# Row maxima of attention scores from a difference and a relu, and exponentials in 32 and 16 bits by key tile

## The chip, the core and the metric

The kernel runs on one core of a Trainium2 chip. The metric is the device time of one execution in microseconds (us); lower is better. The engines are named as the profile names them: PE is TensorE (PEld its weight loads), DVE is VectorE, ACT is ScalarE, POOL is GpSimd, SP is SyncE, which only issues DMAs here. Each engine works through its own queue in program order and waits for others by semaphores.

## The reference

Three layers follow each other. First comes attention inside clusters, then a layer that takes the largest of three products, then a layer of eight experts. The change lies in attention, and touches one buffer of the second layer.

```
q, k, v: (2 batches, 8 heads, 768, 64); centroids: (8 heads, 16, 64)
q_assign = argmax(normalized q @ normalized centroids);  k_assign likewise
scores = where(q_assign == k_assign, q @ k.T / 8, -1e9)
attn = exp(scores - max(scores, -1));  attn /= sum(attn) + 1e-9
x = attn @ v                                  # as (1536, 512)
h = max(x @ w1, x @ w2, x @ w3);  x = h @ w_out        # w: 512 x 768
... experts on x (1536 tokens, 8 experts, 512 -> 1024 -> 512)
```

## The kernel before

**Steps.** Attention is written as 96 steps: 16 heads (batch 0 first, `hp` counts pairs of heads, `j` is 0 or 1 in the pair) times 6 key tiles `kt` of 128 keys. `attention` calls for each step: `tick` (what was put off until now: the maxima of the step before, then small jobs by due time), `scores`, `values` of the step two earlier (`LAG`), the events of that step, and `spare`. What stands first in this program order stands first in each engine's queue.

**Row maxima.** Each step also takes the row maxima of one query tile, 11 steps ahead (`LEAD`): `row_max` has PE multiply one tile of 128 queries with all 768 keys, as two products of 384 into two PSUM banks (line 440), and DVE reduces each bank to one column (L447). The products carry the cluster mask as additional rows of the operands `A` (`Aq`, `Ak`), so a masked key is far below the others. After the sixth tile `shift` (L459 and on) joins the two columns, POOL turns the maxima into 16-bit rows `mq`, and those are turned (by PE or by a DMA) into rows of `Aq`, so that the next product with `Aq` has the maximum already subtracted.

**Scores and values.** `scores` forms the transposed scores of a key tile in two halves of 384 queries, each by two products (L497: the high parts `A`, then the cross terms `C`), and ACT takes the exponential into `p` (L500). For `j = 0` the values are multiplied in 32 bits: `values` issues six products of `p` with 65 columns of `v` (each shows as two rows of the trace). For `j = 1` ACT makes a 16-bit copy `ph` (L510), DVE the remainder `pl` (L511, issued in the next step), and `values` issues 18 16-bit products. All collect in the bank `acc`; `norm` divides (L557 to L560).

**Preparation of a pair.** `prep` returns named jobs: `qk` loads, `Hk`, `Hq`, `Lk`, `Lq` split q and k in 16-bit halves, `ck` and `cq` score the clusters, `f1`, `f2`, `f3` pick the first best cluster (`f1` and `f3` on POOL, L347 and L356 to L359), `mk` and `mq` bring the mask rows into `Ak` and `Aq`, `lv` loads v, `vh` halves it, `pv` has PE sum v over all keys (`totals`, six 32-bit products, L408). The table `CF['T']` gives the step of each job, relative to the pair's first step; `CF['E']` gives other steps for the first two pairs.

**What lies between.** During batch 1's steps one unit of the second layer is issued per step (`UP`; a unit is 12 products of 384 columns, L810, then DVE's maximum L818), and its weights are unpacked from 64-bit words, by three of their pieces per step (`QN`): DVE L718 to L742, ACT L720 and L738, POOL L722 and L737. The rest of the second layer and the experts follow when attention has ended.

**PSUM.** Eight banks: row maxima use three in turn in batch 0 and two from step 53 on, scores two.

Of the kernel before, what the change touches and what calls it, by code (L numbers as in the profile page):

```python
# [22 lines left out]
       'Lk': -26,  # L23
       'Lq': -25,
       'ck': -24,
       'cq': -23,
       'ha': -20,
       'mk': -16,
       'mq': -18,
       'lv': -8,  # L30
       'vh': -3,
       'pv': 5,
       'f1': -19,
       'f2': -19,
       'f3': -19},
 'E': [{'Hk': -29,
# [22 lines left out]
        'mq': -7}],  # L59
# [23 lines left out]
 'LAG': 2}  # L83
# [10 lines left out]
C_SGN = 128  # L94
# [13 lines left out]
def constants():  # L108
# [22 lines left out]
class Kernel:  # L131
# [145 lines left out]
    def prep(self, st):  # L277
# [68 lines left out]
        def first1():  # L346
            nc.gpsimd.tensor_tensor(c["eq"], c["eq"], rk, op=ALU.mult)  # L347
# [5 lines left out]
        def first3():  # L353

            eq = c["eq"]
            nc.gpsimd.tensor_tensor(eq, b16(c["mr"]), rk, op=ALU.subtract)  # L356
            nc.gpsimd.tensor_scalar(eq[:, :2 * NT], eq[:, :2 * NT], 0.0, -1.0, op0=ALU.is_equal, op1=ALU.add)
            for i, dst in enumerate((self.AK, self.AQ)):
# [3 lines left out]
                    (61440.0, 0.0)[i], (0.0, 61440.0)[i], op0=(ALU.mult, ALU.is_equal)[i], op1=(ALU.add, ALU.mult)[i])  # L362
# [22 lines left out]

        def load_v():

            st["v"] = v = self.pl.tile([128, NT, 129], F32, tag="v", name=f"v{nm}")
            nc.gpsimd.memset(v[:, :, 64:65], 2.0 ** -10)
            src = I["vP"][b, hp].rearrange("p (t j d) -> p t j d", t=NT, j=2)  # L390
            for j in range(2):
                nc.sync.dma_start(out=v[:, :, 65 * j:65 * j + 64], in_=src[:, :, j, :])


        def v_halves():
            v = st["v"][:, :, 65:129]
# [13 lines left out]

        def split(pv):
            vsh = self.sm.tile([128, 129], F16, tag="vsh", name=f"vsh{nm}", bufs=1)
# [41 lines left out]
    def shift(self, st, j, m2):  # L454
# [3 lines left out]
        mx = self.sm.tile([128, NT], F32, tag="mx", name=f"mx{nm}", bufs=1)  # L458
        nc.vector.tensor_tensor(mx, m2[:, :, 0], m2[:, :, 1], op=ALU.max)  # L459
# [8 lines left out]
            mq[:, :, j, 40:42], mx.unsqueeze(2).to_broadcast([128, NT, 2]), -(2.0 ** 32), (1.0, 1024.0)[j],  # L468
# [19 lines left out]
    def scores(self, st, j, kt, between):  # L488
# [35 lines left out]
    def values(self, st, j, kt, p, plo):  # L524
# [3 lines left out]
        A = st["A"]  # L528
# [944 lines left out]
```

## Time and profile before

| | us |
|---|---|
| median of 3 runs | 552.56 (548.95 to 554.25) |
| the profiled execution | 551.87 |
| its span, first to last instruction | 550.0 |
| PE busy | 475.8 (87%) |
| DVE busy | 424.2 (77%) |
| ACT busy | 289.0 (53%) |
| POOL busy | 140.2 (25%) |

Busy time is the union of an engine's instructions. A product of PE appears with its whole length, from its first column in to its last result out, so products overlap in the trace and a busy PE isn't a PE at its peak; what a step takes from PE is read from start to start. "Idle before" is the time that an engine stood before instructions of a group, and the releaser is what ended it. The mean granted clock of TensorE was 0.974.

### The profile page before, as it was taken

Reading aid. Unit: us, or ns where it says so; the run is one execution under the profiler, and the core shown is the slowest. Engines: PE = TensorE matmul, PEld = TensorE weight load, DVE = VectorE, ACT = ScalarE, POOL = GpSimd, SP = SyncE. Lnnn points to the kernel's source line nnn. Section 1 sums busy time; section 2 is a strip of 40 time slices with the busy share of each in tenths; the row PEclk is TensorE's granted clock in tenths of the full one; section 3 lists DMA queues with packets and bytes.
Section 4 is the critical chain, followed back from the end, with each engine's and each line's share of the span. In section 5 each row is a group of like instructions: output and inputs, shape, how many; then the busy total and the mean of one; then the engine's idle time right before and its main releaser. Section 6 shows DMA issues by size and latency. Waiting matters only on the chain.

```text
span 550.0 us, 11644 instructions
## 1 busy us (share of the span) xinstructions
PE 475.8 (87%) x4518; PEld 326.4 (59%) x4518; DVE 424.2 (77%) x834; ACT 289.0 (53%) x491; POOL 140.2 (25%) x191
## 2 busy tenths in 40 slices
PE   2589898979879879997998899899999999797392
PEld 1258585858657557755775576555666654465271
DVE  5576979797999998999979943462788775989471
ACT  5255757484944744464456444311666632667460
POOL 3513140323145334724433410000000001412122
PEclk9989999999999999999999999899999999989796
DMA  8637494866859334742532133317488843699810
GB/s 223 169 100 179 84 197 95 203 128 138 134 137 226 96 106 124 179 116 61 143 101 82 54 62 69 58 58 288 149 273 267 269 134 114 208 297 342 301 50 14
DMA packets 89835, 82.91 MB, mean 151 GB/s; under 512 B 55200, under 2 KB 72806, under 8 KB 89778
## 3 DMA queue, kind: packets, MB, share of 16 engines
q1 hardware_dynamic: 88082, 78.98, 53.3%
q0 software_dynamic: 976, 1.85, 1.5%
q10 hardware_dynamic: 720, 1.31, 0.6%
q8 instruction: 36, 0.59, 0.5%
q14 instruction: 21, 0.17, 0.1%
HBM read 57.18 MB, written 4.22 MB: 112 GB/s over the span
## 4 chain that ended last, share of the span: by engine, by line
PE 46%; DVE 30%; DMA 10%; issue 7%; POOL 4%; ACT 1%; SPq 0%; POOLq 0%; DVEq 0%
PE h L810 17%; PE acc L534 9%; DVE m L447 8%; PE x L847 7%; PE p L497 4%; DVE pl L511 4%; DMA exa<-out,ixa 4%; PE p L440 2%; DVE wl L742 2%; DVE wma L736 2%; DVE hm L818 2%; DVE wpw L718 1%; DVE e L1077 1%; PE pvs L408 1%; DVE wma L727 1%
## 5 line engine op out<-in xcount | busy, mean ns | idle before, releaser
L500 ACT ACTIVATE p<-p 128x384 f32<-128x384 f32 x192 | 87.9, 487 | 71.6 <-PE p L497 70.9
L447 DVE TENSOR_REDUCE m<-p 128x1 f32<-128x384 f32 x192 | 97.0, 548 | 10.1 <-PE p L440 10.1
L810 PE MATMUL h<-xh,wh 128*128 128x384 f16 x288 | 93.9, 326 | 0.0
L810 PE MATMUL h<-xh,wl 128*128 128x384 f16 x288 | 93.9, 326 | 0.0
L810 PE MATMUL h<-xl,wh 128*128 128x384 f16 x288 | 93.9, 326 | 0.0
L440 PE MATMUL p<-Ak,Aq 128*128 128x384 f16 x192 | 63.3, 338 | 23.2 <-DVE m L447 22.2
L1077 DVE SCALAR_TENSOR_TENSOR e<-est,e 128x1024 f16<-128x1024 f32 x64 | 76.5, 1217 | 0.9 <-ACT e L1074 0.9
L534 PEld LDWEIGHTS acc<-v,p 128*128 128x128 f32 x576 | 70.2, 192 | 8.1 <-issue 3.7
L810 PEld LDWEIGHTS <-wh 128*128 128x128 f16 x576 | 54.9, 99 | 32.8
L534 PE MATMUL acc<-v,p 128*128 128x65 f32 x576 | 69.8, 271 | 1.9 <-issue 1.1
L1074 ACT ACTIVATE e<-est 128x1024 f16<-128x1024 f32 x64 | 64.7, 1049 | 4.7 <-DMA est<-in_moe_w 4.1
L497 PE MATMUL p<-Aq,Ak 128*128 128x384 f16 x192 | 62.9, 328 | 3.1 <-ACT p L500 2.5
L497 PE MATMUL p<-Cq,Ck 128*128 128x384 f16 x192 | 62.9, 328 | 0.0
L511 DVE TENSOR_TENSOR pl<-p,ph 128x768 f16<-128x768 f32 x48 | 48.1, 1003 | 8.4 <-ACT ph L510 8.4
L737 POOL TENSOR_TENSOR wma<-wma,wpw 128x512 f32<-128x512 f32 x24 | 32.4, 1349 | 84.2 <-DVE wma L736 65.8
L818 DVE TENSOR_TENSOR hm<-h,hm 128x384 f32<-128x384 f32 x48 | 26.6, 554 | 28.6 <-PE h L810 26.8
L823 ACT ACTIVATE hh<-hm 128x384 f16<-128x384 f32 x24 | 12.6, 524 | 59.8 <-DVE hm L818 59.8
L510 ACT ACTIVATE ph<-p 128x768 f16<-128x768 f32 x48 | 40.5, 844 | 1.5
L810 PEld LDWEIGHTS <-wl 128*128 128x128 f16 x288 | 28.2, 98 | 18.6
L1116 POOL DMA_INDIRECT exe<-out,ixe x2 | 2.2, 1088 | 132.7 <-DVE me L1112 132.4
L534 PEld LDWEIGHTS <-ph 128*128 128x128 f16 x576 | 23.1, 98 | 19.8 <-issue 11.9
L497 PEld LDWEIGHTS <-Ak 128*128 128x128 f16 x192 | 19.6, 102 | 24.0 <-issue 14.6
(225 smaller groups left out, 869.5 us busy)
## 6 DMA issues: line engine op xcount, KB each, us to landing
est<-in_moe_w SPq DMA_DIRECT2D x64, 512.0 KB, 5.7
wst<-in_moe_w SPq DMA_DIRECT2D x18, 512.0 KB, 3.8
rawk<-in_kT SPq DMA_DIRECT2D x8, 384.0 KB, 4.6
rawq<-in_qT SPq DMA_DIRECT2D x8, 384.0 KB, 4.1
v<-in_vP SPq DMA_DIRECT2D x16, 192.0 KB, 4.1
wsto<-in_moe_w_out SPq DMA_DIRECT2D x6, 512.0 KB, 3.1
Ak<-Hk SPq DMA_DIRECT2D x16, 96.0 KB, 7.4
Aq<-Hq SPq DMA_DIRECT2D x16, 96.0 KB, 3.0
```

Of the source, the lines that this page charges most:

```text
L440: nc.tensor.matmul(pb[:, :384], lhsT=Aq[:, j, 128 * n:128 * n + 128], rhs=Ak[:, j, 384 * u:384 * u + 384], start=True, stop=True)
L447: nc.vector.reduce_max(m2[:, n, u:u + 1], pbs[u][:, :384], axis=AX.X)
L497: nc.tensor.matmul(pb[:, :384], lhsT=T["k"][:, j, ks], rhs=T["q"][:, j, 384 * u:384 * u + 384], start=first, stop=not first)
L500: nc.scalar.activation(p[:, u], pb[:, :384], AF.Exp, scale=2.0 ** -19)
L510: nc.scalar.activation(ph, p, AF.Copy)
L511: self.low_p = lambda: nc.vector.tensor_tensor(plo, p, ph, op=ALU.subtract)
L534: nc.tensor.matmul(o, lhsT=l, rhs=r, start=start, stop=stop, skip_group_check=True)
L810: nc.tensor.matmul(ps[:, :384], lhsT=l, rhs=r[:, k, :], start=(k == 0 and i == 0), stop=(k == self.NK - 1 and i == 2))
L818: nc.vector.tensor_tensor(new, ps[:, :384], old, op=ALU.max)
L847: nc.tensor.matmul(ps, lhsT=l[:, q], rhs=r, start=(f == 0 and i == 0), stop=(f == 5 and i == 2))
L1074: nc.scalar.activation(hi, st, AF.Copy, scale=64.0)
L1077: nc.vector.scalar_tensor_tensor(lo, st, 64.0, hi, op0=ALU.mult, op1=ALU.subtract)
```

## The change

The larger of two scores a and b is taken as relu(a - b) + b. The keys' operand for the first product becomes `D`, the difference of the first and the second half of `Ak` (a new job `d0`, `d1` per head, on POOL, for the first pair on DVE). ACT takes the relu of that product into an SBUF tile `mh`, and one DVE operation adds the second product to it and writes the maximum of the 384 sums into `mx`. The 16-bit halves are no longer made for all key tiles of `j = 1`: they are made for odd `kt` below `2 * KB[b]`, in both heads of a pair, that is for two of six key tiles in batch 0 and three of six in batch 1. v is scaled by 1024 on POOL (`sv`), summed over its six tiles on POOL (`vt`), so `totals` is one product of 130 columns. `f1` and `f3` go to DVE, where `f3` is one comparison; POOL's form of the mask rows of `aq` is now multiply and add. The second layer's running maximum is kept in place in one of two buffers, where it had a new one of three. The steps of several jobs move.

```diff
@@ CF
-       'mk': -16,
-       'mq': -18,
-       'lv': -8,
+       'mk': -18,
+       'mq': -17,
+       'lv': -10,
+       'sv': -7,
+       'vt': -7,
+       'pv': -5,
        'vh': -3,
-       'pv': 5,
...
+       'f1': -20,
+       'f2': -20,
+       'f3': -19,
+       'd0': -14,
+       'd1': -8},
...
+ 'KB': [2, 3]}
@@ prep
+        def differences(j):
+            k = A["k"]
+            st["D", j] = D = self.pl.tile([128, 384], F16, tag="D", name=f"D{nm}_{j}")
+            (nc.vector if nm == "0_0" else nc.gpsimd).tensor_tensor(
+                D, k[:, j, 0:384], k[:, j, 384:768], op=ALU.subtract)
...
-            nc.gpsimd.tensor_tensor(c["eq"], c["eq"], rk, op=ALU.mult)
+            nc.vector.tensor_tensor(c["eq"], c["eq"], rk, op=ALU.mult)
...
-            nc.gpsimd.tensor_tensor(eq, b16(c["mr"]), rk, op=ALU.subtract)
-            nc.gpsimd.tensor_scalar(eq[:, :2 * NT], eq[:, :2 * NT], 0.0, -1.0, op0=ALU.is_equal, op1=ALU.add)
+            nc.vector.tensor_tensor(eq, b16(c["mr"]), rk, op=ALU.is_equal)
...
+        def scale_v():
+            v = st["v"].rearrange("p n j c -> p (n j c)")
+            nc.gpsimd.tensor_scalar(v, v, 1024.0, None, op0=ALU.mult)
...
+        def sum_tiles():
+            v = st["v"].rearrange("p n j c -> p n (j c)")
+            c["vs"] = t = self.sm.tile([128, 768], F32, tag="x", name=f"vt{nm}", bufs=1)[:, :390].rearrange(
+                "p (n c) -> p n c", n=3)
+            nc.gpsimd.tensor_tensor(t, v[:, 0:3], v[:, 3:6], op=ALU.add)
+            for n in (1, 2):
+                nc.gpsimd.tensor_tensor(t[:, 0], t[:, 0], t[:, n], op=ALU.add)
...
-            for n in range(NT):
-                nc.tensor.matmul(pv[:, :129], lhsT=v[:, n, 64:65].to_broadcast([128, 128]), rhs=v[:, n],
-                                 start=(n == 0), stop=(n == NT - 1))
+            nc.tensor.matmul(pv[:, :130], lhsT=st["v"][:, 0, 0, 64:65].to_broadcast([128, 128]), rhs=c["vs"][:, 0],
+                             start=True, stop=True)
@@ row_max
-                pb[:, :384], lhsT=Aq[:, j, 128 * n:128 * n + 128], rhs=Ak[:, j, 384 * u:384 * u + 384],
+                pb[:, :384], lhsT=Aq[:, j, 128 * n:128 * n + 128], rhs=(st["D", j], Ak[:, j, 384:768])[u],
                 start=True, stop=True)
-            pbs.append(pb)
+            if u == 0:
+                pbs.append(self.sm.tile([128, 384], F32, tag="mh", name=f"mh{nm}_{n}"))
+                nc.scalar.activation(pbs[0], pb[:, :384], AF.Relu)
+            else:
+                pbs.append(pb)

         def reduce():
-            for u in range(2):
-                nc.vector.reduce_max(m2[:, n, u:u + 1], pbs[u][:, :384], axis=AX.X)
+            nc.vector.tensor_tensor_reduce(
+                pbs[0], pbs[1][:, :384], pbs[0], 1.0, -3.0e38, ALU.add, ALU.max, mx[:, n:n + 1])
@@ scores, values
-        if j == 0:
+        if not self.halved(st, kt):
             return p, None
...
+    def halved(self, st, kt):
+
+        return kt % 2 == 1 and kt < 2 * KB[st["b"]]
```

Three places in the order of the instructions show it. The first is ACT in the sixth head of batch 0 (pair 2, `j = 1`), key tiles 2 and 3, before; `p` is an exponential, `ph` its 16-bit copy, `wh` a weight, `vh` and `Hq` are jobs of later pairs.

```order
L500 ACTIVATE p_2_1_2_1790<-p_2_1_2_0_1791 128x384
L500 ACTIVATE p_2_1_2_1790<-p_2_1_2_1_1798 128x384
L510 ACTIVATE ph_2_1_2_1804<-p_2_1_2_1790 128x768
L738 ACTIVATE wh_0_1114<-wma_1442 128x512
L500 ACTIVATE p_2_1_3_1831<-p_2_1_3_0_1832 128x384
L500 ACTIVATE p_2_1_3_1831<-p_2_1_3_1_1839 128x384
L510 ACTIVATE ph_2_1_3_1845<-p_2_1_3_1831 128x768
```

The same place on ACT in the changed kernel, where `mh` is the relu for a row maximum:

```order
L527 ACTIVATE p_2_1_2_1801<-p_2_1_2_0_1802 128x384
L470 ACTIVATE mh_3_1_1_1809<-p_3_1_1_0_1807 128x384
L527 ACTIVATE p_2_1_2_1801<-p_2_1_2_1_1811 128x384
L769 ACTIVATE wh_0_1140<-wma_1445 128x512
L527 ACTIVATE p_2_1_3_1828<-p_2_1_3_0_1829 128x384
L470 ACTIVATE mh_3_1_2_1835<-p_3_1_2_0_1833 128x384
L527 ACTIVATE p_2_1_3_1828<-p_2_1_3_1_1837 128x384
L537 ACTIVATE ph_2_1_3_1843<-p_2_1_3_1828 128x768
```

A relu now stands between the two exponentials of every step, and the copy `ph` is gone from tile 2. The second place is DVE in the same head, before; `m` are the maxima and `vl`, `Lk` jobs of later pairs.

```order
L447 TENSOR_REDUCE m_3_1_1746<-p_3_1_1_0_1796 128x1
L447 TENSOR_REDUCE m_3_1_1746<-p_3_1_1_1_1802 128x1
L511 TENSOR_TENSOR pl_2_1_2_1805<-p_2_1_2_1790,ph_2_1_2_1804 128x768
L447 TENSOR_REDUCE m_3_1_1746<-p_3_1_2_0_1837 128x1
L447 TENSOR_REDUCE m_3_1_1746<-p_3_1_2_1_1843 128x1
L401 SCALAR_TENSOR_TENSOR vl_3_1867<-v_3_1658,vh_3_1866 128x384
L511 TENSOR_TENSOR pl_2_1_3_1846<-p_2_1_3_1831,ph_2_1_3_1845 128x768
```

The same on DVE in the changed kernel; the operation that adds and takes the maximum is named ISA, and is followed by a second one of one column:

```order
L475 ISA mh_3_1_1_1809,mx_3_1_1749<-p_3_1_1_1_1815,mh_3_1_1_1809 128x384
L475 ISA mx_3_1_1749 128x1
L321 SCALAR_TENSOR_TENSOR Lk_1_1869<-rawk_1_1628,Hk_1_1785 128x768
L475 ISA mh_3_1_2_1835,mx_3_1_1749<-p_3_1_2_1_1841,mh_3_1_2_1835 128x384
L475 ISA mx_3_1_1749 128x1
L422 TENSOR_TENSOR vl_3_1865<-v_3_1560,vh_3_1864 128x256
L538 TENSOR_TENSOR pl_2_1_3_1844<-p_2_1_3_1828,ph_2_1_3_1843 128x768
```

Two reductions of 384 became one operation of 384 and one of a single column, and `pl` comes every second step. The third place is the start of the kernel, the cluster masks of the first pair on POOL, before:

```order
L347 TENSOR_TENSOR ceq_0_258<-ceq_0_258,c_60 128x384
L356 TENSOR_TENSOR ceq_0_258<-cmr_0_262,c_60 128x384
L357 TENSOR_SCALAR ceq_0_258<-ceq_0_258 128x192
L359 TENSOR_SCALAR ak<-ceq_0_258 128x12x32
L359 TENSOR_SCALAR aq<-ceq_0_258 128x12x32
```

and DVE in the changed kernel at that point:

```order
L363 TENSOR_TENSOR ceq_0_258<-pcl_0_202,cmx_0_257 128x384
L366 TENSOR_TENSOR ceq_0_258<-ceq_0_258,c_60 128x384
L370 TENSOR_REDUCE cmr_0_262<-ceq_0_258 128x24
L374 TENSOR_TENSOR ceq_0_258<-cmr_0_262,c_60 128x384
L362 TENSOR_REDUCE cmx_1_320<-pcl_1_267 128x24
L363 TENSOR_TENSOR ceq_1_321<-pcl_1_267,cmx_1_320 128x384
L390 COPY Aq_0_193<-paq_0_333 64x768 x2
L338 TENSOR_TENSOR D_0_0_342<-Ak_0_190 128x384
```

POOL keeps the last two of its five; the others are two operations of DVE in a row with their reduction, and `D` follows the mask copies.

## Rows read from the trace of the kernel before

**Rows 1.** Busy time by stage: start to first exponential, batch 0, batch 1, rest.

```profile
0.00:32.45 32.45, 13.40 (x122) 7.26 (x123) 18.19 (x41) 14.67 (x22) 13.45 (x27) 0.96 0.63 167
32.45:150.76 118.31, 107.28 (x1221) 84.43 (x1220) 99.33 (x198) 76.16 (x139) 31.39 (x59) 1.00 0.69 146
150.76:352.00 201.24, 184.61 (x1713) 129.93 (x1712) 171.99 (x317) 105.49 (x201) 71.39 (x86) 1.00 0.46 110
352.00:550.00 198.00, 170.51 (x1469) 104.75 (x1468) 134.67 (x282) 92.71 (x129) 24.01 (x19) 0.94 0.57 192
```

**Rows 2.** Waits of PE in batch 0: us in total, times, longest.

```profile
PE p L440 <- DVE m L447: 7.6, 9, 1.3
PE p L497 <- ACT p L500: 2.5, 4, 0.8
```

**Rows 3.** Waits of PE in batch 1, same columns.

```profile
PE p L440 <- DVE m L447: 13.3, 16, 1.7
```

**Rows 4.** Busy time of PE, PEld, DVE, ACT, POOL in one head of j 0, then j 1.

```profile
62.10:78.20 16.10, 15.14 (x177) 12.53 (x175) 12.58 (x28) 7.03 (x14) 5.58 (x10) 1.00 0.69 160
78.20:91.20 13.00, 11.60 (x140) 8.62 (x139) 12.12 (x25) 12.23 (x21) 2.21 (x6) 1.00 0.68 124
```

**Rows 5.** The same for two heads of batch 1, j 0 and j 1.

```profile
199.90:228.30 28.40, 27.05 (x250) 20.00 (x250) 26.58 (x54) 11.85 (x25) 13.88 (x16) 1.00 0.58 152
228.30:254.40 26.10, 22.96 (x209) 15.29 (x208) 25.37 (x44) 16.45 (x32) 11.35 (x14) 1.00 0.43 102
```

**Rows 6.** Timeline, PE: first scores of two 32-bit steps in a row (start, us).

```profile
137.21 0.33 PE L497 MATMUL p<-Aq,Ak 128*128 128x384 f16 x1
...
139.47 0.33 PE L497 MATMUL p<-Aq,Ak 128*128 128x384 f16 x1
```

**Rows 7.** Timeline: a 16-bit step on PE, and its two reductions on DVE.

```profile
84.37 0.32 PE L497 MATMUL p<-Aq,Ak 128*128 128x384 f16 x1
...
84.46 1.01 DVE L447 TENSOR_REDUCE m<-p 128x1 f32<-128x384 f32 x2
...
85.88 0.33 PE L497 MATMUL p<-Aq,Ak 128*128 128x384 f16 x1
```

**Rows 8.** Groups by line and form: busy us, mean ns, idle before.

```profile
L447 DVE TENSOR_REDUCE m<-p 128x1 f32<-128x384 f32 x192 | 97.0, 548 | 10.1 <-PE p L440 10.1
...
L500 ACT ACTIVATE p<-p 128x384 f32<-128x384 f32 x192 | 87.9, 487 | 71.6 <-PE p L497 70.9
...
L511 DVE TENSOR_TENSOR pl<-p,ph 128x768 f16<-128x768 f32 x48 | 48.1, 1003 | 8.4 <-ACT ph L510 8.4
L510 ACT ACTIVATE ph<-p 128x768 f16<-128x768 f32 x48 | 40.5, 844 | 1.5
...
L818 DVE TENSOR_TENSOR hm<-h,hm 128x384 f32<-128x384 f32 x48 | 26.6, 554 | 28.6 <-PE h L810 26.8 <-PE rp L960 1.8
...
L736 DVE SCALAR_TENSOR_TENSOR wma<-wma,wrs 128x512 f32<-128x512 f32 x24 | 16.5, 688 | 0.6 <-POOL wrs L722 0.6
...
L408 PE MATMUL pvs<-v 128*128 128x129 f32 x96 | 12.5, 279 | 0.0
```

**Rows 9.** Timeline from the start: ACT's accumulator read, POOL's masks, first row maxima.

```profile
5.69 0.19 ACT L256 ACTIVATION_READ_ACCUMULATOR cst<-cst 128x1 f32 x1
...
11.95 0.91 POOL L347 TENSOR_TENSOR ceq<-ceq,c 128x384 f16<-128x384 f16 x1 [7.43 <-DVE ceq L344]
...
13.52 0.84 POOL L356 TENSOR_TENSOR ceq<-cmr,c 128x384 f16<-128x384 f16 x1 [0.67 <-DVE cmr L351]
...
15.42 0.51 POOL L359 TENSOR_SCALAR ak<-ceq 128x384 f16<-128x384 f16 x1
15.90 1.50 POOL L359 TENSOR_SCALAR aq<-ceq 128x384 f16<-128x384 f16 x1
...
19.59 1.14 PE L440 MATMUL p<-Ak,Aq 128*128 128x384 f16 x3 [0.65 <-DVE Aq L373]
...
28.71 0.17 DVE L459 TENSOR_TENSOR mx<-m 128x6 f32<-128x6 f32 x1
```

More of the change, by code (lines that the diff above doesn't have):

```diff
@@ L44 @@
         'mq': -19,
+        'd0': -18,
+        'd1': -17,
         'lv': -30,
+        'sv': -13,
+        'vt': -12,
+        'pv': 3,
         'vh': -9},
@@ L304, in low @@
             if nm == "0_1":
-                L[t] = self.pp.tile([128, S], F16, tag="pl", name=f"L{t}{nm}")
+                L[t] = self.pp.tile([128, S], F16, tag="pl", name=f"L{t}{nm}", bufs=2)
             else:
@@ L401, in v_halves @@
-            self.later(1, lambda: nc.vector.scalar_tensor_tensor(
-                vl, v, 1024.0, vh[:, :, 0:64], op0=ALU.mult, op1=ALU.subtract))
+            v = st["v"][:, 1:2 * KB[b]:2]
+            st["vh"] = vh = self.pl.tile([128, NT // 2, 2, 66], F16, tag="vh", name=f"vh{nm}")[:, :KB[b]]
+            st["vl"] = vl = self.pl.tile([128, NT // 2, 2, 64], F16, tag="vl", name=f"vl{nm}")[:, :KB[b]]
+            nc.scalar.activation(vh[:, :, :, 0:65], v, AF.Copy)
+            v = v[:, :, :, 0:64]
@@ L424, in prep @@
             ha=high_a, f1=first1, f2=first2, f3=first3, mk=lambda: masks("k", self.AK), mq=lambda: masks("q", self.AQ),
-            lv=load_v, vh=v_halves, pv=lambda: self.misc(f"pvs{nm}", totals, split))
+            lv=load_v, sv=scale_v, vh=v_halves, vt=sum_tiles, d0=lambda: differences(0), d1=lambda: differences(1), pv=lambda: self.misc(f"pvs{nm}", totals, split))
     FIRST = 33
@@ L433, in row_max @@
         if n == 0:
-            st["m2"] = self.sm.tile([128, NT, 2], F32, tag="m2", name=f"m2{nm}")
-        m2 = st["m2"]
+            st["mx"] = self.sm.tile([128, NT], F32, tag="mx", name=f"mx{nm}")
+        mx = st["mx"]
         pbs = []
@@ L537, in values @@
             q = slice(128 * n, 128 * n + 128)
-            if j == 0:
-                mm(acc[:, n, :], p[:, q], st["v"][:, kt, 0:65], start=(kt == 0 and n == 0))
-            else:
-                mm(acc[:, n, :], p[:, q], st["vh"][:, kt, 0:65], start=(kt == 0 and n == 0))
-                mm(acc[:, n, 0:64], p[:, q], st["vl"][:, kt])
-        if j == 1:
+            if not halved:
+                mm(acc[:, n, :], p[:, q], st["v"][:, kt, j], start=(kt == 0 and n == 0))
+            else:
+                mm(acc[:, n, :], p[:, q], st["vh"][:, kt // 2, j, 0:65])
+                mm(acc[:, n, 0:64], p[:, q], st["vl"][:, kt // 2, j])
+        if halved:
             for n in range(NT):
-                mm(acc[:, n, :], plo[:, 128 * n:128 * n + 128], st["vh"][:, kt, 0:65])
+                mm(acc[:, n, :], plo[:, 128 * n:128 * n + 128], st["vh"][:, kt // 2, j, 0:65])
         if kt < NT - 1:
@@ L811, in hidden_part, with take @@
                                      stop=(k == self.NK - 1 and i == 2))
-            new = self.fp.tile([128, 384], F32, tag="hm", name=f"hm{c}_{f}_{w}", bufs=3)
-            def take(w=w, ps=ps, new=new, old=m):
+            new = m or self.fp.tile([128, 384], F32, tag="hm", name=f"hm{c}_{f}", bufs=2)
+            def take(w=w, ps=ps, new=new):
                 if w == 0:
@@ L817, in take @@
                 else:
-                    nc.vector.tensor_tensor(new, ps[:, :384], old, op=ALU.max)
+                    nc.vector.tensor_tensor(new, ps[:, :384], new, op=ALU.max)
                 if w < 2:
```

66 lines of the change are left out of this document (29 added, 37 removed).

## The prediction

> **What bounds the kernel now.** I read the stages first [rows 1]. The span has four: 32.45 us until the first exponential, 118.31 us for batch 0's 48 steps, 201.24 us for batch 1's, and 198.00 us behind attention. The reader is to see that PE is the busiest engine of both batches (107.28 of 118.31, 184.61 of 201.24) and that DVE is not far behind (99.33 and 171.99). So PE stands 11.0 us in batch 0 and 16.6 us in batch 1, and that idle time, plus what can be taken from PE itself, is what a change can win there.
>
> PE's own waits say who keeps it [rows 2, 3]. Nearly all of it is a row-max product (L440) that waits for a bank that DVE's reductions have not yet left: 7.6 us in batch 0, 13.3 us in batch 1. Waits for an exponential are 2.5 us in batch 0.
>
> Then I looked at single heads. In batch 0 [rows 4] a head of `j = 0` takes 16.10 us with PE at 15.14, while DVE has 12.58 and ACT 7.03: PE is the bound. A head of `j = 1` takes 13.00 us with PE at 11.60, DVE at 12.12, ACT at 12.23: both are nearly full, PE is not. The work is unevenly spread between the two. In batch 1 [rows 5] a head of either kind has DVE above 25 us of 26 to 28; there `j = 0` heads carry the preparation of a pair and `j = 1` heads the remainders `pl`, beside the unpacking of weights.
>
> **The change part by part.**
>
> *PE.* A step in 32 bits takes 2.26 us from start to start (139.47 - 137.21 [rows 6]), a step in 16 bits 1.51 us (85.88 - 84.37 [rows 7]). Batch 0 had 24 of each and gets 32 and 16: 8 x 0.75 = +6.0 us of PE. Batch 1 keeps 24 and 24, only mixed. The sum of v takes 12 passes per pair, 12.5 us for 96 [rows 8], 0.13 each; two passes of nearly the same width remain, so 10 x 0.13 = 1.3 us per pair goes, 5.2 us per batch. Net +0.8 us in batch 0 and -5.2 us in batch 1. The row-max products stay as many and as wide; only their operand differs.
>
> *DVE per row-max tile.* Before: two reductions, 1.01 us together [rows 7]. After: one operation on 384 columns from PSUM and SBUF, and one of a single column. The trace shows neither. For the first the nearest row is L818, the same 384 columns from PSUM and SBUF, 0.554 us [rows 8]; two 32-bit sources in SBUF run at the same pace (L736, 512 columns, takes 0.688: 128 columns more cost 0.134, 1.05 ns each), so I take it as the lower end too. The upper end is half that pace: 0.554 + 384 x 1.05 ns = 0.957. For the second the nearest is ACT's read of its accumulator, 0.19 [rows 9]; its bounds are 0 and 0.19. I take 0.554 + 0.19 = 0.74, a saving of 0.27 us per tile; the ends are a saving of 0.46 and a loss of 0.14.
>
> [...]
>
> *DVE otherwise.* Batch 0 loses 8 remainders of 1.003 us [rows 8]. `f1` and `f3` bring two operations of 384 columns per pair, 0.55 each by L818; four pairs have theirs in batch 0, two in batch 1. DVE in batch 0: 99.3 - 48 x 0.27 - 8.0 + 4 x 1.1 = 82.7. In batch 1, where 37 tiles are left because the maxima run 11 steps ahead: 172.0 - 10.0 + 2.2 = 164.2.
>
> *ACT.* The relu has the shape of the exponential, 0.487 us [rows 8]: +23.4 us in batch 0, against 8 copies `ph` of 0.844, so 76.2 + 23.4 - 6.8 = 92.8 of some 113; in batch 1 105.5 + 18.0 = 123.5 of 190. It hides under PE as long as ACT keeps up: over one pair of heads in batch 0 [rows 4] ACT has 7.03 + 12.23 + 12 x 0.487 - 2 x 0.844 = 23.4 us, DVE 24.70 - 12 x 0.27 - 2.0 + 1.1 = 20.6, PE 26.74 + 1.5 - 1.3 = 26.9. So PE becomes the bound of every head of batch 0 with the next engine 13% below. If that cover is gone, the relu costs what the last rival says.
>
> *Waits.* A relu frees the first bank at once, the fused operation frees the second; behind the fused operation DVE has the same queue as before. In batch 0, with DVE at 82.7, I let three quarters of the 7.6 us go: -5.7. In batch 1 DVE stays at 164 against PE's 179.4, so the two still alternate and I let half of 13.3 go: -6.7. What is late next is the exponential in batch 0 and DVE still in batch 1.
>
> *POOL.* It gives away `f1` and most of `f3` and gets the differences, the scaling and the sums of v. The nearest price of a difference is L347 with 0.91 us [rows 9]. POOL is busy 31 of 118 and 71 of 201 us [rows 1], and each job is due two or more steps before its reader: nothing, or at worst one late `pv` per pair, 8 x 1 us, which widens the range. `D` waits for the mask rows' DMA at the head of POOL's queue; behind it stands `shift`, three steps later.
>
> *The start.* The first row-max product waits for the masks [rows 9]. `f1` (0.91) and POOL's time from 13.52 to 15.42 become two operations of 0.55: -1.7 us. The rows of `aq` took 1.50 in their old form and 0.51 is what `ak` takes in the form that both now have: -1.0. `D` on DVE adds 0.55. So the product moves from 19.59 to about 17.4. From there to the maxima at 28.71 six tiles save 0.27 each, and one relu's delay is added: together some -1. The first exponential comes 3 us earlier; between 2 and 4.5.
>
> *Behind attention* nothing is changed but the buffers of the running maximum, which are wanted again only two groups of three units later: 0.
>
> **Sum**, against the profiled execution of 551.87 us: -3.0 (start), +0.8 - 5.7 = -4.9 (batch 0), -5.2 - 6.7 = -11.9 (batch 1), 0 (rest): -19.8, so 532.1. The median of the runs, 552.56, lies 0.7 above the profiled one, within its spread; I say 532.
>
> **The rivals.**
>
> 1. *The fused operation runs at half pace.* Then DVE loses 0.14 per tile. Batch 0: 99.3 + 6.7 - 8.0 + 4.4 = 102.4, half of the waits stay: +0.8 - 3.8 = -3.0. Batch 1: DVE gains 7.4 us of work in a stage where it already keeps PE waiting: +7.4 - 5.2 = +2.2. Start -1.5. Together -2.3: 549.6, no change that can be told. For it: no row shows this form. Against: L818 and L736 run at full pace.
>
> 2. *Only a quarter of the waits goes.* PE waits at transitions, when DVE has a burst (norm, cluster choice, weights), and a mean saving of 0.27 us doesn't touch a burst. -2.0 start, +0.8 - 1.9 in batch 0, -5.2 - 3.3 in batch 1: -11.6, 540. For it: in batch 1 the heads of `j = 0` keep all of DVE's preparation and now get remainders as well [rows 5].
>
> 3. *All waits go.* -4 at the start, +0.8 - 7.6 - 2.5 in batch 0, -5.2 - 13.3 in batch 1: -31.8, 520. For it: two banks are now freed by two engines, so PE is let go earlier than the saved time says.
>
> 4. *Slower: the relu keeps the exponentials.* ACT works in order, and the relu stands between the two exponentials of each step. In a 16-bit step of batch 0 ACT has 3 x 0.487 + 0.844 = 2.31 us against PE's 1.51. If the excess isn't made up in the next step (2.26 against 1.46), 16 x 0.8 = 12.8 us; and if PE waits out each relu in the 32 others, 15.6 more. With the sum's other terms: 551.9 - 19.8 + 28.4 = 560. It decides from the point at which PE's waits for exponentials pass some 22 us, from 2.5 now [rows 2]. Against: three buffers of `p` and two score banks carry over a step's excess.
>
> That the change doesn't do what it says is hardly open: the operations stand in the order as described; 0.02.
>
> **How the numbers follow.** My forecast, 525 to 539 with 532 as its middle, has 0.53; rival 1 0.09, rival 2 0.17, rival 3 0.13, rival 4 0.06, the last 0.02. About 1%, 5.5 us, is what a measurement of this kernel can tell from no change. Faster by more than that (below 547): 0.53 + 0.17 + 0.13 and a fifth of rival 1, 0.85. Slower (above 558): 0.07, rival 4 and half of the last. Within: 0.08. The range runs from rival 3 at 520 to 546, past rival 2 with POOL's late sums (540 + 6); rivals 1 and 4 and the edges are left out, under 0.2.
>
> **What the changed profile would show.** Right: the fused operation near 0.55 us and its second part below 0.2; L440's successor waits for DVE below 2 us in batch 0 and 7 in batch 1; all heads of batch 0 near 13.5 us with PE above 95%; the first exponential near 29.5. Wrong: a fused operation near 0.95 (rival 1); exponentials as PE's longest wait (rival 4); `pvs` waiting for POOL; a stage behind attention that isn't 198 us, since I count on it to move as a block.

## The result, and the profile after

| | before | after |
|---|---|---|
| median, first measurement | 551.22 us (4 runs) | 535.36 us (4 runs, 528.36 to 538.91) |
| median, measured again | 550.70 us (11 runs) | 533.64 us (6 runs, 529.83 to 539.52) |

The ratio was 0.963 [0.951, 0.975] at first and 0.967 [0.963, 0.971] when measured again: some 18 us faster, where 532 us was forecast. The profiled execution took 538.91 us (span 537.1) with a granted clock of 0.964; this one and the profile taken when it was measured again (539.52 us) are slow runs, which medians take in and ratios leave out, here and in the table of the experiments.

Groups of the changed kernel, by line and form (busy us, mean ns of one, idle before):

```profile
L475 DVE CUSTOM_DVE_ANT_0 mh<-p,mh 128x384 f32<-128x384 f32 x96 | 52.8, 551 | 34.6 <-ACT mh L470 22.5 <-PE p L465 8.3 <-POOL mq L491 1.8
L470 ACT ACTIVATE mh<-p 128x384 f32<-128x384 f32 x96 | 46.7, 488 | 2.8 <-PE p L465 2.6
...
L413 POOL TENSOR_SCALAR v<-v 128x780 f32<-128x780 f32 x8 | 18.6, 2325 | 11.9 <-DMA v<-in_vP 11.6
L338 POOL TENSOR_TENSOR D<-Ak 128x384 f16<-128x384 f16 x14 | 15.1, 1075 | 28.2 <-DMA Ak<-Mk 10.3 <-ACT ph L537 7.4 <-PE p L465 5.0
...
L475 DVE DVE_READ_ACCUMULATOR2_ANT mx<- 128x1 f32 x96 | 7.8, 81 | 0.0
```

One pair of them on DVE, timeline:

```profile
85.28 0.55 DVE L475 CUSTOM_DVE_ANT_0 mh<-p,mh 128x384 f32<-128x384 f32 x1
85.75 0.08 DVE L475 DVE_READ_ACCUMULATOR2_ANT mx<- 128x1 f32 x1
```

The fused operation takes 0.551 us and its second part 0.081. The second begins before the first has ended, so the pair takes 0.55 us from 85.28 to 85.83, against 1.01 for the two reductions [rows 7]. DVE now stands idle before it, and mostly for the relu: in most steps it is no longer DVE that is late.

Busy time by stage of the changed kernel (length, then PE, PEld, DVE, ACT, POOL, PE's granted clock, DMA share, GB/s), with the same borders as [rows 1]:

```profile
0.00:30.47 30.47, 14.00 (x123) 7.90 (x124) 16.70 (x46) 17.82 (x31) 11.27 (x25) 1.00 0.64 178
30.47:152.32 121.85, 114.77 (x1147) 90.09 (x1145) 78.83 (x195) 85.61 (x183) 38.46 (x63) 0.94 0.67 142
152.32:339.60 187.28, 181.12 (x1659) 127.92 (x1658) 161.56 (x309) 117.61 (x238) 81.38 (x90) 0.99 0.48 118
339.60:537.10 197.50, 171.21 (x1469) 105.89 (x1467) 134.52 (x282) 92.86 (x129) 25.20 (x19) 0.94 0.58 193
```

Start -2.0, batch 1 -14.0 and the rest -0.5 against [rows 1]. But batch 0, in which DVE lost 20 us of work, became 3.5 us *longer*, with a granted clock of 0.94 where it had 1.00. These are stages of that one execution.

What PE waited for in batch 0 (first two rows) and, most of it, in batch 1 (last row) of the changed kernel: us in total, times, longest.

```profile
PE p L524 <- DMA Aq<-pm: 4.5, 3, 2.6
PE p L524 <- ACT p L527: 1.3, 5, 0.5
...
PE p L465 <- DVE mx L475: 3.4, 4, 1.5
```

The waits of the row-max products for DVE are gone in batch 0 (7.6 before [rows 2]) and 3.4 in batch 1 (13.3 [rows 3]). A new one has come: the scores wait for a DMA, the one that brings the finished maxima `pm` into rows of `Aq`. Heads three to six of batch 0 in the same columns as the stages:

```profile
58.37:73.36 14.99, 14.05 (x164) 11.14 (x163) 10.14 (x26) 10.33 (x22) 5.12 (x8) 1.00 0.69 169
73.36:86.82 13.46, 13.16 (x130) 10.59 (x129) 9.61 (x23) 10.76 (x23) 4.13 (x9) 1.00 0.70 115
86.82:103.87 17.05, 14.25 (x163) 11.22 (x162) 10.51 (x27) 9.72 (x22) 6.73 (x11) 0.95 0.85 189
103.87:123.49 19.62, 19.32 (x133) 15.21 (x132) 9.63 (x24) 12.12 (x26) 4.11 (x7) 0.70 0.45 75
```

For all of them 13.5 us was forecast, with PE above 95%. The second is like that (13.5 us, 98%), the first takes 15.0 us with PE at 94%, and the next two take 17.0 and 19.6. Around 96 us the timeline of SP's queue shows why (start, us):

```profile
95.53 0.59 SPq L306 DMA_DIRECT2D rawk<-in_kT  x1
96.17 0.44 SPq L306 DMA_DIRECT2D rawq<-in_qT  x1
96.71 0.39 SPq L743 DMA_DIRECT2D wst<-in_moe_w  x1
97.14 0.57 SPq L543 DMA_DIRECT2D Aq<-pm  x1
```

and the timeline of PE at that place:

```profile
100.06 0.35 PE L565 MATMUL acc<-vh,pl 128*128 128x65 f16 x6
103.01 0.50 PE L524 MATMUL p<-Aq,Ak 128*128 128x384 f16 x1 [2.60 <-DMA Aq<-pm]
103.30 0.53 PE L524 MATMUL p<-Cq,Ck 128*128 128x384 f16 x1
```

The small `Aq<-pm` is issued last, behind the loads of the next k, q and a weight. PE stands (has nothing to do) for 2.60 us until it has landed, and its first products behind take 0.50 and 0.53 us, where the same ones take 0.32 elsewhere. The granted clock of that stretch, one row in the columns of the stages:

```profile
102.10:115.80 13.70, 12.79 (x56) 9.96 (x56) 4.71 (x14) 6.07 (x12) 5.71 (x10) 0.50 0.73 127
```

For 13.7 us, from within this stand on, the granted clock was 0.50, where it had been 1.00 in the heads before.

The order on SP's queue isn't new. Before the change the same DMA stood behind the same three loads (the last of them and the DMA, and PE's wait for it):

```profile
101.56 1.39 SPq L712 DMA_DIRECT2D wst<-in_moe_w  x1
103.05 0.56 SPq L516 DMA_DIRECT2D Aq<-pm  x1
```

```profile
PE p L497 <- DMA Aq<-pm: 0.4, 1, 0.4
```

There PE went on at 107.54, 4.5 us after the start of the issue, and had other work until 0.4 us earlier. In the changed kernel it goes on 5.9 us after the start of the issue (97.14 to 103.01), and its other work ends at 100.4.

### The profile page after: what moved, and what is told of

It is laid out like the page before. It is cut to its first block, busy times and chain, and to the rows that moved or that the text cites. A ratio compares the mean times of both kernels' runs of the same rounds, so it can differ in the third digit from the quotient of the medians.

```text
span 537.1 us, 11560 instructions
## 1 busy us (share of the span) xinstructions
PE 481.1 (90%) x4390; PEld 331.8 (62%) x4390; DVE 391.6 (73%) x828; ACT 313.9 (58%) x579; POOL 156.3 (29%) x197
## 4 chain that ended last, share of the span: by engine, by line
PE 56%; DMA 12%; DVE 11%; issue 7%; ACT 6%; POOL 5%; SPq 2%; POOLq 0%; DVEq 0%; ACTq 0%
PE h L841 22%; PE acc L565 12%; PE x L878 8%; PE p L524 7%; DMA exa<-out,ixa 5%; PE p L465 3%; DMA out<-exa,ixa 3%; DVE pl L538 1%; DVE mh L475 1%; DMA rawq<-in_qT 1%; DMA Mq<-aq 1%; DMA Aq<-pm 1%; ACT mh L470 1%; ACT p L527 1%; PE pcl L352 1%
## 5 line engine op out<-in xcount | busy, mean ns | idle before, releaser
L527 ACT ACTIVATE p<-p 128x384 f32<-128x384 f32 x192 | 92.4, 492 | 55.2 <-PE p L524 47.6
L565 PEld LDWEIGHTS acc<-v,p 128*128 128x128 f32 x672 | 85.1, 198 | 8.7 <-issue 3.5
L565 PE MATMUL acc<-v,p 128*128 128x65 f32 x672 | 84.6, 277 | 0.3
L475 DVE CUSTOM_DVE_ANT_0 mh<-p,mh 128x384 f32<-128x384 f32 x96 | 52.8, 551 | 34.6 <-ACT mh L470 22.5
L524 PE MATMUL p<-Cq,Ck 128*128 128x384 f16 x192 | 64.5, 336 | 0.0
L470 ACT ACTIVATE mh<-p 128x384 f32<-128x384 f32 x96 | 46.7, 488 | 2.8 <-PE p L465 2.6
L538 DVE TENSOR_TENSOR pl<-p,ph 128x768 f16<-128x768 f32 x40 | 43.0, 1075 | 2.6 <-ACT ph L537 2.6
L465 PE MATMUL p<-Ak,Aq 128*128 128x384 f16 x96 | 33.7, 351 | 5.6 <-DVE mx L475 3.4
L465 PE MATMUL p<-D,Aq 128*128 128x384 f16 x96 | 33.8, 352 | 1.9 <-DVE D L338 1.6
L537 ACT ACTIVATE ph<-p 128x768 f16<-128x768 f32 x40 | 33.7, 843 | 1.3
```

The costliest lines, as they stand in the source:

```text
L465: nc.tensor.matmul(pb[:, :384], lhsT=Aq[:, j, 128 * n:128 * n + 128], rhs=(st["D", j], Ak[:, j, 384:768])[u], start=True, stop=True)
L470: nc.scalar.activation(pbs[0], pb[:, :384], AF.Relu)
L475: nc.vector.tensor_tensor_reduce(pbs[0], pbs[1][:, :384], pbs[0], 1.0, -3.0e38, ALU.add, ALU.max, mx[:, n:n + 1])
L524: nc.tensor.matmul(pb[:, :384], lhsT=T["k"][:, j, ks], rhs=T["q"][:, j, 384 * u:384 * u + 384], start=first, stop=not first)
L527: nc.scalar.activation(p[:, u], pb[:, :384], AF.Exp, scale=2.0 ** -19)
L537: nc.scalar.activation(ph, p, AF.Copy)
```

## Experiments

In the table stages go by events that every kernel has: from the first exponential (start) to that of batch 1 (batch 0), from there to the first load of an expert's weights (batch 1), and to the end (rest). This last border lies later than that of [rows 1]; by these borders batch 1 is 222.2 us before and 208.1 after. "Clock low" is the longest stretch, in us, at a granted clock of 0.50 within attention. Stages are of the profiled execution, medians and ratios of the timed ones.

| kernel | median us | ratio to before | start | batch 0 | batch 1 | rest | clock low |
|---|---|---|---|---|---|---|---|
| before | 550.7 to 553.3 | 1 | 32.4 | 118.3 | 222.2 | 177.0 | 3.4 |
| r1_again (the changed kernel) | 533.64 | 0.967 [0.963, 0.971] | 30.3 | 122.2 | 208.1 | 177.1 | 13.7 |
| e2_dve_copy | 529.52 | 0.962 [0.956, 0.967] | 30.6 | 110.5 | 212.4 | 175.0 | 3.4 |
| e4_copy_b0 | 526.28 | 0.953 [0.951, 0.956] | 31.3 | 110.6 | 206.0 | 175.9 | none |
| e8_copy_dma_earlier | 529.20 | 0.956 [0.949, 0.963] | 30.2 | 111.0 | 209.1 | 176.9 | 3.4 |
| e11_before_copy | 553.94 | 1.001 [0.997, 1.004] | 32.4 | 119.3 | 222.9 | 177.3 | 3.4 |
| e1_two_reductions | 543.60 | 0.975 [0.968, 0.981] | 29.7 | 124.0 | 217.0 | 176.2 | 17.1 |
| e5_two_reductions_copy | 539.06 | 0.976 [0.972, 0.980] | 30.1 | 115.0 | 215.0 | 176.8 | 3.4 |
| e7_halves_by_head | 536.97 | 0.971 [0.968, 0.975] | 30.8 | 113.9 | 214.4 | 176.1 | 3.4 |
| e6_three_halves | 522.31 | 0.945 [0.941, 0.949] | 30.6 | 108.1 | 207.7 | 173.5 | 3.4 |
| e3_relu_twice | 545.56 | 0.990 [0.986, 0.994] | 32.7 | 126.8 | 211.1 | 177.5 | 3.4 |
| e9_masks_on_pool | 544.14 | 0.984 [0.977, 0.991] | 34.6 | 116.8 | 214.8 | 176.7 | 17.1 |
| e10_sum_on_pe | 532.68 | 0.967 [0.962, 0.972] | 30.4 | 115.8 | 206.1 | 177.3 | none |

### Where batch 0's gain went: the row of maxima

First the changed kernel once more, without an edit.

> The changed kernel once more, for a profile without the long half-clock stretch that the first one had in batch 0 (13.65 us in its fifth and sixth head). If that stretch is an accident of the one execution, batch 0 takes about 115 us or less here and the whole 526 to 532 us. If it follows from the 2.6 us wait for the DMA of the maxima rows (Aq<-pm) that stands right before it, the wait and a half-clock stretch after it come again in the same head, and the time is 532 to 539 us.

The stand came back (2.6 us at 100.8), and so did the low clock behind it (from 102.6, 13.7 us; the granted clock of batch 0 is 0.94 again). So neither is an accident of one execution. But both traces are of executions at the upper end of this kernel's times, with a granted clock of 0.964; the eight others had 0.964 to 0.982. An estimate: 13.7 us at half the clock take 0.013 from the mean over a span of 537 us, so an execution without this stretch would show some 0.977. By that the long low clock comes in some executions of the kernel and not in all.

Three kernels bring the maxima's row into `Aq` in another way. `AW` says for each batch who does it (0 is DVE with a copy, 2 a DMA), `PW` how many steps after the transpose it is issued.

e2 has the copy in both batches:

```diff
- 'AW': [2, 2],
+ 'AW': [0, 0],
```

e4 has it in batch 0 alone, and e11 is the same edit in the kernel before:

```diff
- 'AW': [2, 2],
+ 'AW': [0, 2],
```

e8 keeps the DMA and changes only its step:

```diff
- 'PW': 3,
+ 'PW': 2,
```

> The changed kernel with the turned maxima rows copied into Aq by DVE, where SP issued a DMA behind the large loads in its queue. Theory (what is left to win in batch 0 is the wait for that DMA): no wait for Aq<-pm on PE, batch 0 at 108 to 113 us, the whole 524 to 530 us. Rival (the exponentials on ACT set the pace of batch 0): within 2 us of the changed kernel. Rival (DVE's queue is held by the copy, which waits for the turning DMA): 537 us or more, with row-max waits.

> The changed kernel with DVE's copy of the maxima rows in batch 0 alone, and the DMA as before in batch 1, where DVE has no time to spare. Theory: batch 0 as with the copy everywhere (110.5 us), batch 1 as in the changed kernel (208 us from its first exponential to the first load of an expert's weights, against 212 with the copy everywhere); 522 to 528 us. Rival (the copy's gain is only an undisturbed clock, the DMA did not matter): a half-clock stretch of 10 us or more in batch 0 again, 530 to 537 us.

> The changed kernel with the DMA of the maxima rows issued one step earlier (PW 2 in place of 3), which puts it ahead of the loads of k, q and a weight in SP's queue and changes nothing on another engine. Theory (the row waits behind these loads): no wait of 2 us or more for Aq<-pm in batch 0, no long half-clock stretch there, batch 0 at 110 to 113 us, the whole 525 to 530 us. Rival (the turning DMA itself or POOL's rows are late, and only an engine's copy avoids it): the wait stays, 531 to 539 us.

> The kernel before with DVE's copy of the maxima rows in batch 0, nothing else. Theory (the late DMA is a wait that the change made, PE waited 0.4 us for it before): within 3 us of the kernel before, 548 to 555 us. Rival (the copy is worth as much without the change): 540 to 545 us.

In e8 the same DMA is issued one step earlier, and so ahead of the loads. SP's queue in e8, timeline:

```profile
94.71 0.56 SPq L543 DMA_DIRECT2D Aq<-pm  x1
95.32 0.58 SPq L306 DMA_DIRECT2D rawk<-in_kT  x1
```

All that PE then waited for in batch 0 of e8, and its stage:

```profile
PE p L524 <- ACT p L527: 1.5, 5, 0.5
```

```profile
30.20:141.20 111.00, 108.50 (x1147) 85.68 (x1146) 79.63 (x195) 85.32 (x184) 38.58 (x63) 1.00 0.74 156
```

PE is busy 108.50 of 111.00 us there. The 4.5 us of waits for the row are gone, no low clock is left in batch 0, and it takes 11 us less than in the changed kernel's profile. Heads five and six together take 28.5 us instead of 36.7: 2.6 us of the difference is the stand, so some 5.5 us is the low clock, in those executions that have it. In the timed runs e8 gains 1.1 points of ratio on the changed kernel and e4 1.3 (6 to 7 us), less than the 11 us between the profiles; how often the low clock comes in those isn't seen, since they have no trace. The copy is worth nothing (e11) in the kernel before, whose PE waited only 0.4 us for the row. DVE's copy in batch 1 as well (e2) gives part of the gain back: batch 1 takes 6.4 us more than in e4. That this is because DVE is still nearly full there was expected, not tested.

What makes the low clock that long stays open. The traces show it behind a stand of PE for this row in the changed kernel (2.6 us, twice), in e1 (2.5 us, then 17.1 low) and in e9 (2.8, 17.1). But a stand of 3.3 us in batch 1 of e5 was followed by 3.4 us of it (the stage has a granted clock of 0.99), one of 3.4 us in e1 by 6.8 (0.98), and one of 2.6 us at the start of the changed kernel, for the masks, by none (1.00).

### Are both halves needed? The fused operation, and the spread of the 16-bit tiles

e1 takes the old row maxima back into the changed kernel, e5 into e4:

```diff
-                rhs=(st["D", j], Ak[:, j, 384:768])[u],
+                rhs=Ak[:, j, 384 * u:384 * u + 384],
...
-            nc.vector.tensor_tensor_reduce(
-                pbs[0], pbs[1][:, :384], pbs[0], 1.0, -3.0e38, ALU.add, ALU.max, mx[:, n:n + 1])
+            for u in range(2):
+                nc.vector.reduce_max(m2[:, n, u:u + 1], pbs[u][:, :384], axis=AX.X)
```

> The changed kernel with the old row maxima: two products with the halves of the keys and two reductions on DVE, no relu, no differences. Theory (both parts needed: the fused operation lets PE go): PE's waits for DVE at the row-max products come back, some 3 us in batch 0 and 10 us or more in batch 1; 541 to 548 us. Rival (the even spread of the 16-bit halves does it all): 533 to 537 us, as the changed kernel.

> The kernel of the run before with the old row maxima (two products with the halves of the keys, two reductions on DVE, no relu). Beside that run this is what the fused operation is worth when no late DMA disturbs it. Theory: DVE has 0.4 us more per tile, and PE's waits at the row-max products come back in batch 1 (10 us or more) and hardly in batch 0, where DVE has room: 6 to 14 us above it, 530 to 538 us. Rival (the even spread of the halves is the whole gain): within 2 us of it.

e1 has the stand and 17.1 us of low clock too, so its batch 0 says little, and I put the question again on e4, which has neither. e5 is 12.8 us slower than e4: 4.4 in batch 0, 9.0 in batch 1. PE's first wait in batch 0 and in batch 1 of e5:

```profile
PE p L462 <- DVE m L469: 5.4, 13, 0.7
...
PE p L462 <- DVE m L469: 12.3, 13, 3.3
```

These are the waits that the change was to remove, not far below what they were before (7.6 and 13.3 [rows 2, 3]); in batch 0 hardly any had been expected.

e7 is e4 with the 16-bit halves for all key tiles of `j = 1` again, as before (`vh` and `vl` get six tiles of one head):

```diff
-        if not self.halved(st, kt):
+        if not j:
...
-        A, halved = st["A"], self.halved(st, kt)
+        A, halved = st["A"], j == 1
```

e6 is e4 with three alternate tiles of six in batch 0 too:

```diff
- 'KB': [2, 3]}
+ 'KB': [3, 3]}
```

> The kernel with the copy in batch 0, and the 16-bit halves by head again (all key tiles of j = 1, none of j = 0) beside the fused operation; the halves keep two buffers, which can add a wait of ACT. Theory (the even spread is needed, or the relu overloads ACT in heads of j = 1): those heads of batch 0 take 15 us or more against 13.4 and wait for exponentials, the others 14; batch 0 at 116 us or more, the whole 8 us or more above. Rival (the fused operation alone frees PE): within 3 us of the kernel with the copy.

> The kernel with the copy in batch 0, and KB = [3, 3]: three of six key tiles of batch 0 in 16 bits instead of two, so 8 steps of batch 0 take 0.75 us less of PE and 0.84 and 1.0 us more of ACT and DVE. Theory (PE is the bound of batch 0): batch 0 falls by 3 to 6 us, to 105 to 108, the whole by as much. Rival (ACT is as near as PE): batch 0 within 1.5 us of 110.5, with waits for exponentials.

e7 is 10.7 us slower than e4, 3.3 of it in batch 0 and 8.4 in batch 1. The work is the same in batch 1, and only its order differs. PE's first wait in batch 1 of e7, and below it that of e4:

```profile
PE p L465 <- DVE mx L475: 9.9, 10, 2.5
```

```profile
PE p L465 <- DVE mx L475: 4.5, 6, 1.5
```

So an even spread is a gain of its own: in batch 1 DVE's remainders no longer come in one head out of two.

e6 and e7 have the same 24 tiles in 16 bits in both batches, so between them little but the order differs: e7 is 14.7 us slower, 5.8 of it in batch 0 (108.1 us spread evenly, 113.9 by head) and 6.7 in batch 1. What PE waits for most in batch 0 of e7, and below it the same in e6:

```profile
PE p L524 <- ACT p L527: 6.0, 6, 1.2
```

```profile
PE p L524 <- ACT p L527: 2.1, 6, 0.5
```

There it is ACT that the even spread relieves, which by head has the copies `ph` and the relu in the same steps.

And e6 against e4 says what eight steps in 32 bits cost in batch 0: 2.5 us, just below the 3 to 6 that were expected. PE's busy time falls by 4.5 us, but it stands 2.0 us more. e6 is the fastest kernel here, 0.945 of the time before and 4 us below e4 (part of that lies behind attention, where nothing was changed): at KB = 2 PE is the bound of batch 0 (106.82 busy of 110.60) and the 16-bit steps still fit on DVE and ACT. Stage rows of batch 0 in e4, then in e6:

```profile
31.30:141.90 110.60, 106.82 (x1144) 84.82 (x1142) 81.95 (x201) 85.31 (x184) 38.46 (x63) 1.00 0.74 154
```

```profile
30.60:138.70 108.10, 102.33 (x1186) 79.29 (x1184) 90.27 (x210) 90.92 (x192) 40.95 (x63) 1.00 0.71 157
```

### How near is ACT? The relu twice

```diff
-                nc.scalar.activation(pbs[0], pb[:, :384], AF.Relu)
+                for _ in range(2):
+                    nc.scalar.activation(pbs[0], pb[:, :384], AF.Relu)
```

> The changed kernel with each relu done twice, 96 more activations of 0.49 us on ACT. Theory (the relu hides under PE): ACT goes from 85.6 to 109 us in batch 0, near PE, so the time rises by 2 to 8 us, nearly all in batch 0. Rival (ACT's order, the relu between the exponentials, already sets the pace): each step grows by a relu, 0.41 us, +20 to +40 us, in both batches.

2.3 points of ratio more than the changed kernel, some 13 us, between the two expectations. PE's largest wait in batch 0 of e3, and the stage:

```profile
PE p L525 <- ACT p L528: 8.2, 19, 0.7
```

```profile
32.70:159.50 126.80, 114.12 (x1144) 87.42 (x1143) 79.37 (x195) 109.15 (x235) 38.71 (x63) 0.97 0.62 136
```

With one relu PE waits 1.3 to 1.5 us for exponentials, with two 8.2, and batch 0 takes 15.8 us more than in e8 (2.1 of it are waits for the maxima's row, which is late here as in the changed kernel). ACT need not be full for that: it is busy 109 of 127 us. The first relu is hidden, a second would not be.

### What POOL's work costs: the masks and the sum of v

e9 is e4 with `f1`, `f3` and the rows of `aq` in the form of before, on POOL:

```diff
-            nc.vector.tensor_tensor(c["eq"], c["eq"], rk, op=ALU.mult)
+            nc.gpsimd.tensor_tensor(c["eq"], c["eq"], rk, op=ALU.mult)
...
-            nc.vector.tensor_tensor(eq, b16(c["mr"]), rk, op=ALU.is_equal)
+            nc.gpsimd.tensor_tensor(eq, b16(c["mr"]), rk, op=ALU.subtract)
+            nc.gpsimd.tensor_scalar(eq[:, :2 * NT], eq[:, :2 * NT], 0.0, -1.0, op0=ALU.is_equal, op1=ALU.add)
```

e10 is e4 with the sum of v on PE in twelve passes, and without POOL's additions:

```diff
-            nc.tensor.matmul(pv[:, :130], lhsT=st["v"][:, 0, 0, 64:65].to_broadcast([128, 128]), rhs=c["vs"][:, 0],
-                             start=True, stop=True)
+            for n in range(NT):
+                nc.tensor.matmul(pv[:, :130], lhsT=st["v"][:, n, 0, 64:65].to_broadcast([128, 128]),
+                                 rhs=st["v"][:, n].rearrange("p j c -> p (j c)"), start=(n == 0), stop=(n == NT - 1))
```

> The kernel with DVE's copy in batch 0, and the choice of the first best cluster on POOL again in its old form (f1, f3). Theory: the first exponential comes 2 to 3 us later (33.5 against 31.3) and the rest stays within 2 us, so 527 to 531 us. Rival (it was moved for POOL's sake, which is now late with differences, sums of v and maxima rows): 6 us or more above 526.3, with waits of PE for POOL's results or for the maxima rows.

> The kernel with DVE's copy in batch 0, and v summed over its six tiles by PE again, in 12 passes per pair, with no sums on POOL. Theory (PE is the bound, each pass counts): +1.2 us per pair, 8 to 10 us in all, 534 to 537 us. Rival (the sums on POOL cost as much by being late): within 2 us of 526.3.

e9 is 17.9 us slower than e4 (the kernel before was 0.6 slower beside it, too), as its rival said: 3.3 at the start, 6.2 in batch 0, 8.8 in batch 1. Before the second batch the timeline of POOL in e9 reads:

```profile
134.75 0.88 POOL L429 TENSOR_TENSOR vt<-v 128x390 f32<-128x390 f32 x1 [1.45 <-DVE x L615]
135.71 0.95 POOL L431 TENSOR_TENSOR vt<-vt 128x130 f32<-128x130 f32 x2
136.62 1.01 POOL L374 TENSOR_TENSOR ceq<-cmr,c 128x384 f16<-128x384 f16 x1
137.72 0.87 POOL L375 TENSOR_SCALAR ceq<-ceq 128x192 f16<-128x192 f16 x1
138.67 0.51 POOL L377 TENSOR_SCALAR ak<-ceq 128x384 f16<-128x384 f16 x1
139.15 1.50 POOL L377 TENSOR_SCALAR aq<-ceq 128x384 f16<-128x384 f16 x1
140.73 0.26 POOL L490 TENSOR_SCALAR ok<-mx 128x6 f32<-128x6 f32 x1
```

`ok`, the first operation on a head's maxima, comes without idle time behind seven operations on v and the masks. The masks are late as well, and so are all the DMAs behind them; SP's queue, and PE at the end of it, in e9:

```profile
142.39 1.21 SPq L513 DMA_TRANSPOSE pm<-mq  x1
143.65 1.28 SPq L513 DMA_TRANSPOSE Mq<-aq  x1
145.02 1.90 SPq L544 DMA_DIRECT2D Ak<-Mk  x2
147.69 1.10 SPq L544 DMA_DIRECT2D Aq<-Mq  x2
148.88 0.58 SPq L544 DMA_DIRECT2D Aq<-pm  x1
...
150.82 0.34 PE L525 MATMUL p<-Aq,Ak 128*128 128x384 f16 x1 [2.83 <-DMA Aq<-pm]
```

PE stands 2.83 us before the first scores of batch 1 (by the borders of the table the stand still counts to batch 0), and from 151.9 the clock is low for 17.1 us (granted clock 0.52 from 151.4 to 168.5). At half the clock that costs up to 8.5 us, an estimate, so the low clock can be nearly all of what batch 1 lost. At these steps POOL has no room for the masks beside the sums: `f1` and `f3` on DVE are what lets the sums stand there. What the masks on POOL cost without the low clock behind them isn't shown.

e10 is 6.4 us slower than e4 (5.2 in batch 0, 0.1 in batch 1), less than the 8 to 10 that were expected. Five of the eight sums fall in batch 0 (PE has 50 rows more there, ten for each sum), so a sum costs 1.0 us where PE is the bound. The three in batch 1 cost nothing: PE's busy time there rises from 197.88 to 200.83 us while the stage stays, as the stage rows of batch 1 in e4 and in e10 show, and PE's waits for DVE at the row-max products fall from 4.5 to 1.9 us.

```profile
141.90:347.90 206.00, 197.88 (x1838) 137.44 (x1836) 173.75 (x372) 121.02 (x246) 81.22 (x90) 1.00 0.45 112
```

```profile
146.20:352.30 206.10, 200.83 (x1868) 140.84 (x1867) 171.02 (x373) 121.22 (x246) 75.23 (x81) 1.00 0.45 112
```

## Why the prediction was right, and what in it was not

The time came out as forecast, 535.4 and 533.6 against 532, by the mechanism that was named: the row-max products no longer wait for DVE's reductions. That the total came so near is in part luck: a late DMA took 6 to 7 us that the sum didn't have, and an even spread of work gave what the sum didn't have either. Term by term:

- *The fused operation* was taken at 0.74 us, with its second part behind it at 0.19. It is 0.551, and the second part (0.081) ends with it. So the saving is 0.46 us per tile by these rows, and 0.40 by DVE's busy time in batch 0 of e5 and e4 (100.92 and 81.95 us, 48 tiles), where 0.27 was taken and 0.46 was the upper end. DVE in batch 0 was put at 82.7 us and is 78.8. Full pace, so rival 1 is out: with one source in PSUM and an accumulator the operation takes 0.551 us, no more than the 0.554 of L818 without one [rows 8]. The upper end that I gave it, half of that pace (0.957 us), was an assumption of mine that no run shows. Nor does a run show the operation with both sources in SBUF and an accumulator; without one, L736 takes 0.688 us for 512 columns [rows 8].
- *The waits.* Forecast: -5.7 in batch 0 and -6.7 in batch 1. Gone: 7.6 and 9.9. Undone alone (e5 against e4) the step costs 4.4 and 9.0.
- *Batch 0* was forecast at -4.9 and came out at +3.5 in the profiled execution, with the long low clock in it. The step that failed is "What is late next is the exponential in batch 0": next was the DMA of the maxima's row (4.5 us of waits), for which PE waited 0.4 us before and which I did not follow along SP's queue, though `shift` feeds it. With that DMA one step earlier and nothing else changed (e8) batch 0 is -7.3 and the whole span -22.8, against -19.8 in the sum.
- *Eight more steps in 32 bits* were put at +6.0; e6 against e4 shows 2.5 in batch 0. PE's work was 4.5 of them, and part of that was hidden.
- *The even spread* has no term in the sum at all, though I had seen that the work "is unevenly spread between the two". Undone (e7) it is worth 10.7 us against e4, and 14.7 against e6, which has the same steps in 16 bits.
- *The sum of v* was put at -5.2 in each batch. Undone (e10) it is worth 5.2 in batch 0, which has five of the eight sums, and 0.1 in batch 1. So batch 1's total was near (-11.9 forecast, -14.0 measured) with a wrong split: there it is the fused operation and the spread that count, and PE's saving doesn't, since its waits for DVE grow by nearly as much.
- *POOL* was put at nothing, and this held, but only because the masks left it: the 38.5 us that POOL has in batch 0 are harmless, the 57.9 of e9 are not. I had counted `f1` and `f3` on DVE, with the new form of `aq`'s rows, as -2.7 at the start and as DVE's load; undone alone they are worth 17.9, of which up to 8.5 is the low clock in the traced execution.
- *The start* was put at -3.0, and is -2.0 (30.47). *The rest* moved as a block: 197.5 against 198.0.
- *Rival 4* (the relu holds the exponentials) is out: PE waits 1.3 us for them in batch 0, less than the 2.5 before [rows 2], and ACT is busy 85.6 us there where 92.8 was reckoned. e3 shows that the margin is less than a second relu.

Single steps don't add. Undone one at a time on e4, the fused operation, the spread, the sum and the masks cost 12.8, 10.7, 6.4 and 17.9 us, 47.8 together, and all of the gain of e4 is 26.4. I take it that each undone step alone makes one engine late again and wastes what the others saved; no run undoes two of them on e4.

## What to carry to other kernels

When the wait that holds the busiest engine goes, follow what that wait had been hiding along every in-order queue: here a small DMA behind three loads, 0.4 us of waiting before, kept about a quarter of the gain (6 to 7 us of some 25), and issuing it one step earlier gave that back. Where two engines take turns at being full, spreading the same work evenly can be worth nearly as much as making it cheaper (10.7 us here, beside 12.8 for the fused operation). And a saving on an engine is worth its size only in the stage which that engine sets (5.2 us in batch 0 and 0.1 in batch 1 for the sum of v): ask it stage by stage.

## What the runs showed of the hardware

- A stand of PE can cost more than its length: with the 2.6 us for the maxima's row came 13.7 us of a granted clock of 0.50 in both traces of the changed kernel, by estimate some 5.5 us of further loss. Other stands of 2.6 to 3.4 us had up to 6.8 us of it behind them, or none.
- DVE's read of its accumulator took 0.081 us and ended with the operation before it (85.75 to 85.83); ACT's took 0.19 [rows 9].
- On POOL the scaling of 780 columns in 32 bits took 2.3 us, and 384 columns in 16 bits 1.08 us, where DVE took 0.35 for the same difference in the first pair.
